# Moving attention steps, weight sums and raw loads by a slot or more, and shifting operand addresses by 32 bytes, in a hand-ordered attention + two-layer MLP kernel

## The chip, the cores and the metric

The kernel runs on one core of a Trainium2 chip. The metric is the device time of one execution in microseconds. The kernel before takes 1599.51 us (median of 3 runs, 1598.06 to 1600.45). Engines are named as in the profile: PE is TensorE, PEld its weight loads, DVE is VectorE, ACT is ScalarE, POOL is GpSimd, SP is SyncE, whose queue here issues most DMAs.

## The reference, cut to what matters

Three stages run one after the other on 4608 rows (8 batches of 576 positions; 8 heads of 64 make 512 columns):

```python
# attention without a score matrix: softmax of q over the head's 64, of k over the 576 positions
q_s = exp(q - max_d q); q_s /= sum_d q_s + 1e-9
k_s = exp(k - max_s k); k_s /= sum_s k_s + 1e-9
x = q_s @ (k_s^T @ v)                      # -> (4608, 512)
# layer 1
h = x @ w_in;  x = (max(h, 0)**2) @ w_out  # 512 -> 2048 -> 512
# layer 2, other weights
h = x @ w_in2; g = where(h > 0, h, exp(min(h, 0)) - 1)
out = g @ w_out2                           # 512 -> 2048 -> 512
```

All of it is float32. The kernel keeps that precision by splitting each operand into a high part (as the matmul rounds it) and the rest: a product is three matmuls, hi x hi, lo x hi and hi x lo.

## The kernel before, in words

The 4608 rows are nine blocks of 512 columns (`TB`). For each block the attention makes x, layer 1 makes h in 16 columns of 128 (`up`, 12 matmuls of 512 each), and then y (`down`). Block 0 runs `up` and `down` by turns and converts the first layer's weights meanwhile. From block 1 on (`PAIRED`), two blocks are a pair: the first block's `up`, the second block's `up`, and then one combined w_out product in 56 units of six matmuls (`u_mm`), a Strassen-like scheme with seven products in place of eight that needs sums and differences of w_out's quarters. Those are made on the chip by `w_join` and `s_first` to `s_lo`, eight groups in the order `FREED`, and stored to DRAM (`w1s`) for `u_load`. The raw weights of layer 2 are loaded in blocks 3 to 8 (`w_load`), put together (`w_scale`, `w_fields`, `w_sign`) and treated in the same way (`w2s`, `w3s`). Layer 2 then runs over five stretches of columns (512, 512, 512, 384, 384): 56 products of six matmuls each in a first phase (`product`, L839: x's halves stream past the weights), and 56 units in a second (`d_mm`, L944: g's halves are the weights and w2 streams).

The order of the work is written out by hand. Every engine does its own instructions strictly in the order in which the program gives them, and waits at the head of its queue. The program's clock is the slot: `(t, "u", j)` is the end of column j of block t, `(0, "c", s)` a half column of block 0, `(t, "s", u)` two units of the combined product. `attention(t)` gives 32 lists of steps, in the order in which they depend on each other; `place_all` spreads these lists over slots, and the loops over `FREED` and over the weights add the sums and the loads by a counter `at` into a list `late` of slots. When a slot comes, its steps are issued on their engines in the order in which they were placed.

What the steps are called: `q_norm` (L367) is the last step on q for one of four row groups; `x_tr` (L380) transposes all four groups of q for one pair of heads, so that it needs the fourth `q_norm`; `x_mm` (L405) multiplies that with `kvs`; `kv_mm` (L288) makes `kvs` for one pair of heads. `xl` and `xh` (L422, L423) are x's two parts for the next block's `up`, `x_split`. `psh` has two PSUM buffers: `up` of column j+2 needs ACT's eviction of column j (L570).

Buffers that the change touches: `st`, four tiles of 2 KB that the sums (`s_hi`, `s_lo`), `y_out` and two `u_load`s share; `raw`, three tiles that raw weights and sums take by turns; `w2`, a ring of nine tiles for layer 2's weights; and the tiles of x's parts (`x2_split`) and g's parts (`d_split`) in layer 2. The last are 64 elements larger than their data, and the data starts at an offset that differs from tile to tile: 32 bytes times the operand's number for x, 0, 64 or 128 bytes for g's high parts, and 32 more for the low ones.

Of the kernel before, what the change touches and what calls it, by code (L numbers as in the profile page):

```python
# [20 lines left out]
def tile_attention_moe_moe2(  # L21
# [171 lines left out]
    def s_hi(w, j, k):  # L193
        hi = pool.tile([P, DM], F32R, tag="st", bufs=4, name=f"sh{w}_{j}_{k}").rearrange("p (i n) -> p i n", n=HW)
        if k == 3:
            nc.scalar.activation(hi[:, 0], s_alone(w, j)[0], AF.Copy)
        else:
            x, d = s_source(w, j, k)
            nc.scalar.activation(hi, x, AF.Copy)
            nc.gpsimd.dma_start(d[:, :, 0, :], f32(hi))  # L200
        parts[w, j, k] = hi

    def s_lo(w, j, k):
# [5 lines left out]
        else:  # L209
            x, d = s_source(w, j, k)  # L210
            lo = pool.tile([P, DM], F32R, tag="st", bufs=4, name=f"sl{w}_{j}_{k}").rearrange("p (i n) -> p i n", n=HW)
# [223 lines left out]
    def attention(t):  # L435
# [6 lines left out]
        for b in new:  # L442
            for p in range(NP):
                for i, f in (
# [3 lines left out]
                    put(i + 4 * p, f, b, p)  # L448
# [7 lines left out]
        turns = ((25, 28), (26, None), (29, 31), (30, None)) if far else ((23, 26), (24, None), (27, 29), (28, None))  # L456
# [128 lines left out]
    def down(layer, t, j):  # L585
# [3 lines left out]
        for c in range(NP):  # L589
# [6 lines left out]
            if last and t < NB - 1:  # L596
                y_out(t, c, pool.tile([P, TB], F32, tag="st", bufs=4, name=f"o{layer}_{t}_{c}"))
# [53 lines left out]
    def u_load(t, u):  # L651
        if u < NU:
            i, j = SEVEN[u // NG][0], u % NG
            tag, bufs = ("at", 2) if u < 2 else ("st", 4) if u < 4 else (("xh", "xl")[u % 2] + str(u % 8 // 2), 1)
# [96 lines left out]
    RING = 9  # L751
# [37 lines left out]
    def shifted(pool, tag, bufs, name, n, o):  # L789

        t = pool.tile([P, 2 * TB + 64], F32R, tag=tag, bufs=bufs, name=name)
        return t[:, o : o + 2 * SIZES[n]].rearrange("p (i n) -> p i n", i=2)
# [3 lines left out]
    def x2_split(n, i):  # L796
        x = xq[n, OPERANDS[i]]
        hi = shifted(early2, f"xh{i}", 1, f"x2h{n}_{i}", n, 8 * i)
        lo = shifted(early2, f"xl{i}", 1, f"x2l{n}_{i}", n, 8 * i)
# [257 lines left out]
    with tc.manual_schedule():  # L1057
# [23 lines left out]
        place_all(x[2:], firsts[PAIRED][:-2])  # L1081
# [19 lines left out]
        late = [(0, "c", s) for s in (NSL - 2, NSL - 1)]  # L1101
        late += sorted(firsts[1] + firsts[1][1::2], key=lambda x: x[2]) + firsts[2][:6]
# [150 lines left out]
```

## Time and profile before

| What | us |
|---|---|
| Median of 3 runs | 1599.51 |
| The profiled execution | 1603.41 |
| Its span, first to last instruction | 1601.5 |
| Around the span (1603.41 - 1601.5) | 1.9 |
| PE busy | 1549.7 (97%) |
| DVE busy | 1227.0 (77%) |
| ACT busy | 1026.0 (64%) |

The profile is of one execution. Busy times of PE overlap (a matmul's recorded time is longer than the distance to the next one's start), so that PE's rate is read from the distance between starts. The stretches of the program, by the starts of their first matmuls: block 0 from 32.7 us, block 1 from 133.9, block 2 from 203.6, the pair's combined product 250.9 to 333.2, blocks 3 and 4 from 333.2, 5 and 6 from 520.2, 7 and 8 from 707.8, the last combined product 805.1 to 882.7, and layer 2 from there to 1597.5, with phases of 77.9 and 80.3 us for 512 columns.

### The profile page before, as it was taken

What the parts mean: (1) busy time and instruction counts of PE and PEld (TensorE: products, weight loads), DVE (VectorE), ACT (ScalarE), POOL (GpSimd) and SP (SyncE); (2) the same over time, 40 slices, a digit from 0 to 9 for tenths busy, and PEclk for the clock granted to TensorE, in tenths of its full rate; (3) what the DMA queues carried; (4) which work ended last, traced back from release to release, by engine and by line L of the source; (5) the groups of instructions that cost most, each with busy time, mean ns of one, the idle gap of its engine ahead of it and who ended that gap; (6) DMA issues with size and microseconds to landing.
All of it is one profiled execution on the core that took longest, in us unless ns stands there. A gap on an engine that the chain in (4) does not pass through costs nothing.

```text
span 1601.5 us, 25635 instructions
## 1 busy us (share of the span) xinstructions
PE 1549.7 (97%) x9046; PEld 1328.0 (83%) x9046; DVE 1227.0 (77%) x1795; ACT 1026.0 (64%) x1648; POOL 107.5 (7%) x214
## 2 busy tenths in 40 slices
PE   5999799999999999999999999999999999999999
PEld 3777587877877777787878889988998899999999
DVE  7986676787878868686488688868876887787786
ACT  7986555567655765666556685478547854875863
POOL 0001220013101230012200000000000000000000
PEclk9999999999999999999999999999999999999999
DMA  9856664856668775656277676777677767888877
GB/s 238 249 173 210 225 233 144 273 191 229 223 183 272 244 248 196 199 198 219 115 253 240 181 241 183 224 204 243 181 224 203 229 183 226 269 273 277 262 238 221
DMA packets 203647, 352.99 MB, mean 220 GB/s; under 512 B 20224, under 2 KB 67328, under 8 KB 203520
## 3 DMA queue, kind: packets, MB, share of 16 engines
q1 hardware_dynamic: 192000, 313.60, 64.3%
q0 software_dynamic: 11520, 37.76, 5.9%
q8 instruction: 73, 1.20, 0.3%
q14 instruction: 54, 0.44, 0.1%
HBM read 288.36 MB, written 62.91 MB: 219 GB/s over the span
## 4 chain that ended last, share of the span: by engine, by line
PE 59%; issue 19%; DVE 11%; ACT 4%; DMA 3%; POOL 2%; SPq 0%; POOLq 0%; DVEq 0%; ACTq 0%
PE p L839 19%; PE y L944 17%; PE p L678 8%; PE ph L562 4%; PE ph L561 4%; PE ph L563 4%; DVE dl L925 2%; DVE t L899 1%; DVE g L903 1%; ACT dh L924 1%; ACT t L890 1%; PE px L405 1%; DVE g L917 1%; PE pt L380 1%; DVE ul L666 1%
## 5 line engine op out<-in xcount | busy, mean ns | idle before, releaser
L944 PE MATMUL y<-w,dh 128*128 128x256 f32 x2016 | 359.4, 281 | 0.0
L839 PE MATMUL p<-x2h,w 128*128 128x512 f32 (+1 forms) x1120 | 325.5, 371 | 0.0
L944 PEld LDWEIGHTS y<-w,dh 128*128 128x128 f32 x2016 | 310.2, 188 | 0.1
L944 PE MATMUL y<-w,dl 128*128 128x256 f32 x1008 | 285.9, 284 | 2.5 <-DVE dl L925 2.2
L678 PE MATMUL p<-uh,w 128*128 128x512 f32 x896 | 282.2, 392 | 0.0
L561 PE MATMUL ph<-xh,wi0h 128*128 128x512 f32 x576 | 232.7, 404 | 4.3 <-ACT B L570 3.6
L839 PEld LDWEIGHTS p<-x2h,w 128*128 128x128 f32 x1120 | 207.3, 188 | 29.5
L562 PE MATMUL ph<-xl,wi0h 128*128 128x512 f32 x576 | 227.4, 395 | 2.0 <-DVE xl L423 1.9
L563 PE MATMUL ph<-xh,wi0l 128*128 128x512 f32 x576 | 227.3, 395 | 1.8 <-DVE wi0l L146 1.8
L839 PE MATMUL p<-x2l,w 128*128 128x512 f32 (+1 forms) x560 | 207.8, 371 | 0.0
L678 PEld LDWEIGHTS p<-uh,w 128*128 128x128 f32 x896 | 168.2, 188 | 36.2 <-issue 1.5
L944 PEld LDWEIGHTS y<-w,dl 128*128 128x128 f32 x1008 | 190.3, 189 | 5.3 <-DVE dl L925 4.8
L665 ACT ACTIVATE uh<-B 128x512 fp32r<-128x512 f32 x192 | 121.0, 632 | 100.9 <-PE p L678 69.8
L924 ACT ACTIVATE dh<-g 128x1024 fp32r<-128x1024 f32 (+1 forms) x120 | 115.7, 973 | 101.5 <-PE y L944 100.5
L678 PE MATMUL p<-ul,w 128*128 128x512 f32 x448 | 176.1, 393 | 2.2 <-DVE ul L666 1.7
L666 DVE TENSOR_TENSOR ul<-B,uh 128x512 fp32r<-128x512 f32 x192 | 130.0, 688 | 52.4 <-ACT uh L665 51.3
L925 DVE TENSOR_TENSOR dl<-g,dh 128x1024 fp32r<-128x1024 f32 (+1 forms) x120 | 133.7, 1115 | 42.3 <-ACT dh L924 41.9
L570 ACT ACTIVATE B<-ph 128x512 f32<-128x512 f32 x128 | 75.9, 593 | 113.9 <-PE ph L563 113.1
L561 PEld LDWEIGHTS ph<-xh,wi0h 128*128 128x128 f32 x576 | 110.8, 192 | 33.9 <-ACT B L570 6.2
L563 PEld LDWEIGHTS ph<-xh,wi0l 128*128 128x128 f32 x576 | 109.5, 190 | 25.9 <-DVE wi0l L146 2.2
L562 PEld LDWEIGHTS ph<-xl,wi0h 128*128 128x128 f32 x576 | 109.9, 191 | 25.4 <-DVE xl L423 3.3
L839 PEld LDWEIGHTS p<-x2l,w 128*128 128x128 f32 x560 | 105.2, 188 | 14.5
(133 smaller groups left out, 2277.2 us busy)
## 6 DMA issues: line engine op xcount, KB each, us to landing
w<-w2s SPq DMA_DIRECT2D x280, 256.0 KB, 3.1
w<-w3s SPq DMA_DIRECT2D x280, 256.0 KB, 3.0
w<-w1s SPq DMA_DIRECT2D x224, 256.0 KB, 3.6
raw_wo<-wo_dram SPq DMA_DIRECT2D x32, 512.0 KB, 4.2
ks<-k_dram SPq DMA_DIRECT2D x32, 320.0 KB, 5.1
vr<-v_dram SPq DMA_DIRECT2D x32, 320.0 KB, 6.1
kt<-kt_dram SPq DMA_DIRECT2D x32, 288.0 KB, 4.4
q<-q_dram SPq DMA_DIRECT2D x36, 256.0 KB, 4.9
```

The source lines that it names most:

```text
L380: nc.tensor.transpose(pt[:, s * P : (s + 1) * P], st["q", t, s][:, 2 * p : 2 * p + 2, :].rearrange("p h d -> p (h d)"), ident,)
L561: nc.tensor.matmul(ph, hi[:, c], xh[p], start=(p == 0), stop=False)
L562: nc.tensor.matmul(ph, hi[:, c], xl[p], start=False, stop=False)
L563: nc.tensor.matmul(ph, lo[:, c], xh[p], start=False, stop=(p == NP - 1))
L570: nc.scalar.activation(g, ph, AF.Relu)
L665: nc.scalar.activation(hi, x, AF.Copy)
L666: nc.vector.tensor_tensor(lo, x, f32(hi), op=ALU.subtract)
L678: nc.tensor.matmul(accs[side, m], w[:, s, m], x, start=(new and (j, s) == (0, 0) and x is hi), stop=(j == NG - 1 and s == 1), skip_group_c ...
L839: nc.tensor.matmul(acc, w[:, s, c], x[:, k], start=(begin and (k, s) == (0, 0) and x is hi), stop=((k, s) == (1, 1)), skip_group_check=not ...
L924: nc.scalar.activation(hi, x, AF.Copy)
L925: nc.vector.tensor_tensor(lo, x, f32(hi), op=ALU.subtract)
L944: nc.tensor.matmul(y2[side, b][:, a * HW : (a + 1) * HW], x[:, u % 2, at], w[:, s], start=(new and (j, s, a) == (0, 0, 0) and x is hi), st ...
```

## The change

It has five parts. (1) Attention for block 1: the last `kv_mm` and the first `x_tr` come a half column later in block 0. Attention for block 2: its last seven lists are no longer spread evenly over block 1, but put on given columns. (2) w_out's sums: one step a slot over block 1 and block 2's first 14 columns, where block 1 had one step in even and two in odd columns and block 2 only six. (3) Layer 2's raw weights: `w_load` a slot later, and no weight steps in the last two columns of blocks 3, 5 and 7; what stood there moves on. (4) `st` has five buffers and the ring `w2` eleven. (5) x's parts in layer 2 have tiles of just their size, which start at multiples of 128 bytes; g's parts all start 32 bytes after a multiple of 64.

```diff
     def s_hi(w, j, k):
-        hi = pool.tile([P, DM], F32R, tag="st", bufs=4, name=f"sh{w}_{j}_{k}").rearrange("p (i n) -> p i n", n=HW)
+        hi = pool.tile([P, DM], F32R, tag="st", bufs=5, name=f"sh{w}_{j}_{k}").rearrange("p (i n) -> p i n", n=HW)
...
-                    put(i + 4 * p, f, b, p)
+                    put(i + 4 * p + (not far and i == 11 and p == NP - 1), f, b, p)
...
-        turns = ((25, 28), (26, None), (29, 31), (30, None)) if far else ((23, 26), (24, None), (27, 29), (28, None))
+        turns = ((25, 28), (26, None), (29, 31), (30, None)) if far else ((24, 26), (24, None), (27, 29), (28, None))
...
-    RING = 9
+    RING = 11
...
-    def shifted(pool, tag, bufs, name, n, o):
-
-        t = pool.tile([P, 2 * TB + 64], F32R, tag=tag, bufs=bufs, name=name)
-        return t[:, o : o + 2 * SIZES[n]].rearrange("p (i n) -> p i n", i=2)
+    def shifted(tag, name, n):
+
+        t = pool2.tile([P, 2 * TB + 16], F32R, tag=tag, bufs=3, name=name)
+        return t[:, 8 : 8 + 2 * SIZES[n]].rearrange("p (i n) -> p i n", i=2)
...
-        hi = shifted(early2, f"xh{i}", 1, f"x2h{n}_{i}", n, 8 * i)
-        lo = shifted(early2, f"xl{i}", 1, f"x2l{n}_{i}", n, 8 * i)
+        hi = early2.tile([P, 2, SIZES[n]], F32R, tag=f"xh{i}", name=f"x2h{n}_{i}")
+        lo = early2.tile([P, 2, SIZES[n]], F32R, tag=f"xl{i}", name=f"x2l{n}_{i}")
...
-        hi = shifted(pool2, "gh", 3, f"dh{n}_{q}", n, 16 * (q % 3))
-        lo = shifted(pool2, "gl", 3, f"dl{n}_{q}", n, 16 * (q % 3) + 8)
+        hi = shifted("gh", f"dh{n}_{q}", n)
+        lo = shifted("gl", f"dl{n}_{q}", n)
...
         place_all(x[:2], [(0, "c", NSL - 2)])
-        place_all(x[2:], firsts[PAIRED][:-2])
+        place_all(x[2:25], firsts[PAIRED][:-5])
+        for s, steps in zip((0, 0, 0, 1, 2, 2, 3), x[25:]):
+            place_all([steps], firsts[PAIRED][NFC - 5 + s :])
...
-        late = [(0, "c", s) for s in (NSL - 2, NSL - 1)]
-        late += sorted(firsts[1] + firsts[1][1::2], key=lambda x: x[2]) + firsts[2][:6]
+        late = [(0, "c", s) for s in (NSL - 2, NSL - 1)] + firsts[1] + firsts[2][:-2]
...
             if t % 2:
-                late += firsts[t]
+                late += firsts[t][:-2]
...
-                    for d, f in ((0, w_load), (3, w_scale), (4, w_fields), (5, w_sign)):
+                    for d, f in ((1, w_load), (3, w_scale), (4, w_fields), (5, w_sign)):
```

Three places where the order of instructions changes. PE, block 0, around column 12 (`pk` is `kv_mm`'s result, `pt` that of `x_tr`, `ph` that of `up`). Before:

```order
L595 MATMUL y_0_3_563<-gh_0_9_1059,wo_9_1082 128x512
L288 MATMUL pk_3_1202<-vr_3_1003,ks_3_1000 64x65 x10
L380 MATMUL pt_0_1225<-ident,q_0_452 128x128
L380 MATMUL pt_0_1225<-ident,q_1_454 128x128
L380 MATMUL pt_0_1225<-ident,q_2_462 128x128
L380 MATMUL pt_0_1225<-ident,q_3_468 128x128
L561 MATMUL ph_0_12_1235<-xh_0_0_384,wi0h_1115 128x512
L562 MATMUL ph_0_12_1235<-xl_0_0_397,wi0h_1115 128x512
```

The same place now, behind the whole of column 12's `up`:

```order
L562 MATMUL ph_0_12_1210<-xl_0_3_423,wi0h_1115 128x512
L563 MATMUL ph_0_12_1210<-xh_0_3_416,wi0l_1116 128x512
L288 MATMUL pk_3_1228<-vr_3_1003,ks_3_1000 64x65 x10
L380 MATMUL pt_0_1252<-ident,q_0_452 128x128
L380 MATMUL pt_0_1252<-ident,q_1_454 128x128
L380 MATMUL pt_0_1252<-ident,q_2_462 128x128
L380 MATMUL pt_0_1252<-ident,q_3_468 128x128
L380 MATMUL pt_1_1259<-ident,q_0_452 128x128
```

The product `pk_3` and the transposes `pt_0` have moved from ahead of column 12's twelve matmuls to behind them, next to `pt_1`.

DVE, block 1, ahead of the fourth `q_norm` (`q_3<-q_3,qz_3`), which the first `x_tr` needs; `mt_wo_j` is `w_join` of row group j of w_out, `sumswo` and `slwo` are the sums and their low parts. Before:

```order
L176 TENSOR_TENSOR sumswo_7_1841<-mt_wo_15_1836,sumswo_7_1841 128x256
L212 TENSOR_TENSOR slwo_7_1_1888<-sumswo_7_1841,shwo_7_1_1885 128x512
L354 TENSOR_REDUCE qz_3_1908<-q_3_1462 128x8
L359 TENSOR_SCALAR qz_3_1908<-qz_3_1908 128x8
L212 TENSOR_TENSOR slwo_7_2_1914<-sumswo_7_1841,shwo_7_2_1911 128x512
L153 TENSOR_TENSOR mt_wo_0_1917<-wo_0_464 128x512
L153 TENSOR_TENSOR mt_wo_8_1919<-wo_8_1008 128x512
L303 TENSOR_SCALAR kz_3_1952<-pk_3_1940 64x1
L304 TENSOR_SCALAR kz_3_1952<-pk_3_1940 64x1
L315 RECIPROCAL kz_3_1952<-kz_3_1952 128x1
L363 RECIPROCAL qz_3_1908<-qz_3_1908 128x8
L367 TENSOR_TENSOR q_3_1462<-q_3_1462,qz_3_1908 128x512
```

The same place now:

```order
L176 TENSOR_TENSOR sumswo_6_1815<-mt_wo_14_1779,sumswo_6_1815 128x256
L212 TENSOR_TENSOR slwo_6_1_1862<-sumswo_6_1815,shwo_6_1_1859 128x512
L354 TENSOR_REDUCE qz_3_1884<-q_3_1462 128x8
L212 TENSOR_TENSOR slwo_6_2_1889<-sumswo_6_1815,shwo_6_2_1886 128x512
L359 TENSOR_SCALAR qz_3_1884<-qz_3_1884 128x8
L303 TENSOR_SCALAR kz_3_1921<-pk_3_1909 64x1
L304 TENSOR_SCALAR kz_3_1921<-pk_3_1909 64x1
L315 RECIPROCAL kz_3_1921<-kz_3_1921 128x1
L363 RECIPROCAL qz_3_1884<-qz_3_1884 128x8
L367 TENSOR_TENSOR q_3_1462<-q_3_1462,qz_3_1884 128x512
L153 TENSOR_TENSOR mt_wo_7_1927<-wo_7_936 128x512
L153 TENSOR_TENSOR mt_wo_15_1929<-wo_15_1406 128x512
```

The sums have reached group 6 here, where they had reached the first step of group 0 (the fifth in the order 4, 5, 6, 7, 0, ...) before: ten DVE instructions fewer stand ahead of that `q_norm` in block 1 (two pairs of L153, four sums, two low parts).

DVE at the start of block 4 (`xl_4_p<-xf_4,xh_4_p` are the low parts that block 4's first `up` needs; `mt_wi_3` and `slwi_2` are steps on layer 2's weights). Before:

```order
L207 TENSOR_TENSOR shwi_2_3_3986<-mt_wi_10_3912,shwi_2_3_3986 128x256
L212 TENSOR_TENSOR slwi_2_1_4011<-sumswi_2_3948,shwi_2_1_4008 128x512
L126 SCALAR_TENSOR_TENSOR mt_wi_3_4014<-raw_wi_3_3882 128x512
L423 TENSOR_TENSOR xl_4_0_4021<-xf_4_0_3909,xh_4_0_4020 128x512
L423 TENSOR_TENSOR xl_4_1_4028<-xf_4_0_3909,xh_4_1_4027 128x512
```

The same place now:

```order
L176 TENSOR_TENSOR sumswi_2_3948<-mt_wi_2_3848,sumswi_2_3948 128x256
L207 TENSOR_TENSOR shwi_2_3_3984<-mt_wi_10_3910,shwi_2_3_3984 128x256
L423 TENSOR_TENSOR xl_4_0_4013<-xf_4_0_3907,xh_4_0_4012 128x512
L423 TENSOR_TENSOR xl_4_1_4020<-xf_4_0_3907,xh_4_1_4019 128x512
L423 TENSOR_TENSOR xl_4_2_4027<-xf_4_2_3980,xh_4_2_4026 128x512
```

The low part `slwi_2_1` and `mt_wi_3` no longer stand between block 3's work and block 4's `xl`; blocks 6 and 8 start in the same way.

## Rows read from the trace of the kernel before

**Rows 1.** The page: busy time of each engine.
```profile
PE 1549.7 (97%) x9046; PEld 1328.0 (83%) x9046; DVE 1227.0 (77%) x1795; ACT 1026.0 (64%) x1648; POOL 107.5 (7%) x214
```

**Rows 2.** Timeline of PE, block 0, column 12: start, duration, instruction, idle time before.
```profile
100.80 0.39 PE L595 MATMUL y<-gh,wo 128*128 128x512 f32 x1
102.43 0.80 PE L288 MATMUL pk<-vr,ks 128*64 128x65 f32 x20 [1.24 <-issue]
105.33 0.48 PE L380 MATMUL pt<-ident,q 128*128 128x128 f32 x1 [1.62 <-DVE q L367]
```

**Rows 3.** Stretches: length, busy time (count) by engine, granted clock, DMA share, GB/s.
```profile
105.40:110.70 5.30, 5.30 (x13) 4.06 (x14) 3.44 (x9) 5.07 (x10) 0.00 (x0) 0.50 0.53 158
181.40:186.30 4.90, 4.90 (x13) 3.88 (x14) 1.35 (x4) 0.60 (x1) 0.00 (x0) 0.51 0.06 23
203.60:250.90 47.30, 47.05 (x258) 37.99 (x257) 35.66 (x73) 26.53 (x52) 7.59 (x20) 1.00 0.51 172
707.80:760.60 52.80, 49.92 (x225) 38.88 (x224) 37.39 (x71) 33.01 (x61) 15.07 (x22) 0.97 0.62 217
882.70:960.50 77.80, 77.80 (x337) 63.12 (x336) 56.77 (x60) 61.23 (x76) 0.00 (x0) 1.00 0.73 217
```

**Rows 4.** Timeline of DVE, block 0: the fourth q_norm.
```profile
104.59 0.68 DVE L367 TENSOR_TENSOR q<-q,qz 128x512 f32<-128x512 f32 x1
```

**Rows 5.** Timeline of PE, block 1: its waits.
```profile
165.54 0.50 PE L561 MATMUL ph<-xh,wi0h 128*128 128x512 f32 x1 [1.58 <-ACT B L570]
169.61 0.80 PE L288 MATMUL pk<-vr,ks 128*64 128x65 f32 x20 [1.04 <-issue]
176.73 0.80 PE L288 MATMUL pk<-vr,ks 128*64 128x65 f32 x20 [0.58 <-issue]
181.37 0.48 PE L380 MATMUL pt<-ident,q 128*128 128x128 f32 x1 [3.37 <-DVE q L367]
191.71 0.66 PE L380 MATMUL pt<-ident,q 128*128 128x128 f32 x4 [0.81 <-ACT xf L416]
196.96 1.09 PE L405 MATMUL px<-qt,kvs 64*64 64x128 f32 x14 [1.04 <-ACT qt L386]
```

**Rows 6.** Groups of DVE by line and form: busy us, mean ns, idle before.
```profile
L153 DVE TENSOR_TENSOR mt_wo<-wo 128x512 f32<-128x512 f32 x16 | 10.3, 682 | 0.0
L166 DVE TENSOR_TENSOR sumswo<-mt_wo,mt_wo 128x256 f32<-128x256 f32 x16 | 6.8, 422 | 0.4
L212 DVE TENSOR_TENSOR slwo<-sumswo,shwo 128x512 fp32r<-128x512 f32 x32 | 21.9, 688 | 30.2 <-ACT shwo L199 24.9 <-DMA w3s<-shwo 3.3 <-DMA w1s<-slwo 1.8
```

**Rows 7.** Timeline of PE, blocks 4, 6, 7 and 8: waits.
```profile
388.97 0.50 PE L562 MATMUL ph<-xl,wi0h 128*128 128x512 f32 x1 [0.84 <-DVE xl L423]
574.62 0.50 PE L561 MATMUL ph<-xh,wi0h 128*128 128x512 f32 x1 [0.56 <-ACT xh L422]
738.65 0.33 PE L380 MATMUL pt<-ident,q 128*128 128x128 f32 x1 [1.92 <-DVE q L367]
761.61 0.50 PE L562 MATMUL ph<-xl,wi0h 128*128 128x512 f32 x1 [0.58 <-DVE xl L423]
```

**Rows 8.** DMA issues by line: count, KB, median us to landing.
```profile
raw_wo<-wo_dram SPq DMA_DIRECT2D x32, 512.0 KB, 4.2
```

**Rows 9.** Timeline of PE, layer 2's first products: low parts of the first two.
```profile
882.91 0.39 PE L839 MATMUL p<-x2l,w 128*128 128x512 f32 x1
883.59 0.39 PE L839 MATMUL p<-x2l,w 128*128 128x512 f32 x1
884.28 0.40 PE L839 MATMUL p<-x2l,w 128*128 128x512 f32 x1
884.98 0.40 PE L839 MATMUL p<-x2l,w 128*128 128x512 f32 x1
```

**Rows 10.** Groups of PE, layer 2's second phase, by form.
```profile
L944 PE MATMUL y<-w,dh 128*128 128x256 f32 x2016 | 359.4, 281 | 0.0
L944 PE MATMUL y<-w,dl 128*128 128x256 f32 x1008 | 285.9, 284 | 2.5 <-DVE dl L925 2.2
```

More of the change, by code (lines that the diff above doesn't have):

```diff
@@ L210, in s_lo @@
             x, d = s_source(w, j, k)
-            lo = pool.tile([P, DM], F32R, tag="st", bufs=4, name=f"sl{w}_{j}_{k}").rearrange("p (i n) -> p i n", n=HW)
+            lo = pool.tile([P, DM], F32R, tag="st", bufs=5, name=f"sl{w}_{j}_{k}").rearrange("p (i n) -> p i n", n=HW)
             nc.vector.tensor_tensor(lo, x, f32(hi), op=ALU.subtract)
@@ L596, in down @@
             if last and t < NB - 1:
-                y_out(t, c, pool.tile([P, TB], F32, tag="st", bufs=4, name=f"o{layer}_{t}_{c}"))
+                y_out(t, c, pool.tile([P, TB], F32, tag="st", bufs=5, name=f"o{layer}_{t}_{c}"))
     def y_out(t, c, o):
@@ L653, in u_load @@
             i, j = SEVEN[u // NG][0], u % NG
-            tag, bufs = ("at", 2) if u < 2 else ("st", 4) if u < 4 else (("xh", "xl")[u % 2] + str(u % 8 // 2), 1)
+            tag, bufs = ("at", 2) if u < 2 else ("st", 5) if u < 4 else (("xh", "xl")[u % 2] + str(u % 8 // 2), 1)
             w = pool.tile([P, 2, 2, P], F32R, tag=tag, bufs=bufs, name=f"w1_{t}_{u}")
```

## The prediction

> **What bounds the kernel now.** I read the page's busy times first: PE is busy 97% of the span, DVE 77% [rows 1]. So a microsecond in which PE stands still, or runs at half its clock, is nearly always a microsecond of the end, and work of DVE or ACT costs only where PE has to wait for it. The timeline of PE was therefore searched for idle times in brackets, and the table of stretches for a granted clock under 1. The reader is to see three kinds of loss. In block 0, PE waits 1.24 us ahead of the last `kv_mm` and 1.62 us for the fourth `q_norm` [rows 2]; then thirteen matmuls take 5.30 us at a granted clock of 0.50 [rows 3], which is the 1.2 GHz level. In block 1 there are six waits, the longest of 3.37 us, again for a `q_norm` [rows 5], and behind it 4.90 us at 0.51 [rows 3]. And the second blocks of pairs start late by 0.84, 0.56 and 0.58 us, for `xl` or `xh` [rows 7]. Layer 2 has no wait of that size: what counts there is the distance from one matmul to the next.
>
> The working is made against the profiled execution: 1603.4 us, span 1601.5 and 1.9 around it. It is 3.9 us above the median of 1599.5; the same difference is then taken from the median.
>
> **Part 1a, block 0.** The two waits are 2.86 us. At full clock three matmuls of 512 columns stand 0.68 us apart (882.91 to 883.59) [rows 9], so twelve need 2.72 us; the slow stretch takes 5.30, a loss of 2.6. After the change column 12's twelve matmuls come first: they would start at 101.03 (0.23 behind the L595 of 100.80), end at 103.76, `kv_mm` takes some 0.73 more, and the fourth transpose is due at about 104.7. The fourth `q_norm` ends at 104.59 + 0.68 = 105.27 [rows 4]. A wait of 0.6 stays. Nothing is added: the transposes are the same ones, and `x_mm` for them keeps its slot. I take 2.86 + 2.6 - 0.6 = **-4.9**; if the clock still falls it is -2.3.
>
> **Parts 1b and 2, block 1.** The six waits are 1.58 + 1.04 + 0.58 + 3.37 + 0.81 + 1.04 = 8.4 us [rows 5], and the slow stretch costs 4.90 - 2.72 = 2.2 [rows 3]; 10.6 in all. The first four waits, 6.6 us, come from DVE being late: its sums stand between attention's steps. Ahead of the fourth `q_norm`, ten instructions go: 4 x 0.68 + 4 x 0.42 + 2 x 0.69 = 5.8 us [rows 6]. So 0.8 of the 6.6 stays. The last two, 0.81 and 1.04, are `x_tr` and `x_mm` treading on each other's two PSUM buffers; with a column of twelve matmuls (2.7 us) between them, ACT's copies fit. The second `x_mm` comes a column later, nearer to block 2's `x_split`: I count 0.5 for that. 10.6 - 0.8 - 0.5 = **-9.3**.
>
> The sums aren't gone: two of the eight groups move into block 2. A group costs DVE 2 x 0.68 + 4 x 0.42 + 2 x 0.69 = 4.4 us, so block 2's DVE goes from 35.66 us to about 44.5 of 47.3 [rows 3], 94%. Not shown before: what such a fill costs there. Bounds: 0 (block 2 today has PE busy 47.05 of 47.30) and 8.8 (block 1's DVE waits with their slow clock, all over again). Nearer is block 2 itself, where every step of attention has columns to spare: **+1**.
>
> **Part 3, raw weights.** Ahead of block 4's `xl`, DVE loses one L212 and one L126, about 1.4 us, more than the waits of 0.84, 0.56 and 0.58 [rows 7]; blocks 6 and 8 are alike: **-2.0**. The steps that left the last two columns stand elsewhere, and every later one shifts. Block 7's wait of 1.92 us on a `q_norm` [rows 7] and the clock of 0.97 over 52.8 us there (1.6 us) [rows 3] may go or be copied into block 5. Bounds -7 and +5; with the fifth `st` buffer, which takes away DVE's 3.3 and 1.8 us behind DMAs [rows 6], I take **-2**. A raw load now has two slots, 5.4 us, to land, and a median of 4.2 us [rows 8]: that cover is 1.2 us thick. It was issued into a queue that stood still until DVE freed the buffer, so that it will hardly land later: 0. SP's order behind it (k, v and w1 loads) only gets freer.
>
> **Part 4.** A ring of nine covers nine products of 1.39 us already: 0. The two extra loads stand at the end of a stretch in which PE is full.
>
> **Part 5a, x's parts.** The first product's operand starts at a multiple of 128 bytes, the second's 96 bytes after one: their low parts' triples take 0.68 and 0.70 us [rows 9]. The whole phase runs at 77.8 / 336 = 231.5 ns a matmul [rows 3], the aligned product at 227. If all 1008 matmuls of 512 columns came down to 227, it would be -4.6; if the first product is quick for another reason, 0. No row shows a gain at 384 columns. Midway: **-2.3**. On the Trainium skill, SBUF — State Buffer, "Operand start alignment", an operand need only start at a multiple of its element size, and the same page gives cachelines of 16 bytes, in which 32 is as good a start as 0; by that this term is 0 and the sum 17.2. The pair 0.68 and 0.70 speaks against it, thinly.
>
> **Part 5b, g's parts.** All of them will start 32 bytes off, as only the low parts do now. Matmuls with a low part show 284 ns, with a high one 281 [rows 10]. If 3 ns is the price of an offset, 2016 x 3 = +6 us; if it is the price of going from one offset to the other, 1008 x 3 = -3. Recorded durations are not distances, and both kinds of term are gone if the difference is only in the record: **0**.
>
> **Sum.** -4.9 - 9.3 + 1 - 2.0 - 2 - 2.3 = -19.5: 1583.9 for an execution like the profiled one, **1580.0** for the median.
>
> **Rivals.**
> 1. The clock falls at other waits. For it: a wait of 1.92 us in block 7 is enough company for a fall, and small waits will stay. Against: both long slow stretches come straight behind the longest waits. It gives back 2.6 + 2.2: 1584.8. On the Trainium skill, TensorE: Matmul & The Clock Gate, Part 1, the unit that watches PE runs freely, so that equal work can meet it differently from run to run; no run here shows that yet.
> 2. Block 2 becomes what block 1 was: DVE at 94% of it, PE waiting for `kv_mm` and `x_tr` in its columns 6 to 13. For it: the same steps, the same engine. Against: its attention steps are spread thinner and it has no `down`. It puts back 8.8 in place of 1: 1587.8.
> 3. g's parts at 32 bytes cost their 6 us: 1586.0. For it: 284 against 281; against: it is 1% of a modelled duration.
> 4. Slower: the raw loads. There are 32 in blocks 3 to 8. If each lands after its `w_scale` is due, ACT stands at the head of its queue with the evictions of `ph` behind it, and PE has two buffers. Above 0.61 us of PE a load (19.5 / 32) the gain is gone; at 1 us it is 1580 + 32 = 1612. Against: 5.4 us for 4.2, and ACT is busy 64% [rows 1].
> 5. That the change doesn't do what it says would be an address that is not moved: then part 5 is 0, inside the forecast's range.
>
> **How the numbers follow.** The forecast gets 0.55, with a range of its own of 1574 to 1586; rival 1 0.18, rival 2 0.15, rival 3 0.07, rival 4 0.05. All but the last are well over 0.2% (3.2 us, about what a measurement of this kernel can tell from no change) faster; two together, or rival 2 doubled, could reach 1596.3, for which 0.03 is set aside out of rivals 2 and 3. So faster 0.92, within 0.2% 0.03, slower 0.05. The range of 1571 to 1592 takes in rivals 1 to 3; its lower end has part 3 at -7 and x's parts at -4.6 with a little over (-26.8, 1572.7).
>
> **What would show it.** Right: no bracket of a `q_norm` over 1 us on PE in blocks 0 and 1; granted clock 1.0 from about 100 to 200 us; block 2 starting some 14 us earlier; `xl` and `xh` not named at the starts of blocks 4, 6 and 8; layer 2's first phases of 512 columns at about 77.1 us, the second ones still 80.3. Wrong: brackets of 1 us and more in block 2's columns 6 to 13, or a DMA of raw weights named ahead of L120 on ACT and PE waiting behind; a second phase of 81 us or more; or a clock under 1 at a new place.

## The result: 1585.47 us, 0.9915 of the time before

The changed kernel takes 1585.47 us (median of 4 runs, 1582.64 to 1589.17) against 1599.45 us for the kernel before: a ratio of 0.9915, 95% interval 0.9891 to 0.9938. The forecast was 1580.0, with a range of 1571 to 1592. The profiled execution took 1583.97 us with a span of 1582.0, and the sum made for the profiled execution was 1583.9. That agreement is chance: one term was wrong by 8.7 us and others made up for it. Lengths by the starts of the first matmuls, each profile against its own start:

| Stretch | before | after | difference | the prediction's term |
|---|---|---|---|---|
| block 0 | 101.18 | 104.99 | +3.8 | -4.9 (1a) |
| block 1 | 69.65 | 59.11 | -10.5 | -9.3 (1b and 2) |
| block 2 | 47.29 | 46.72 | -0.6 | +1 |
| combined product behind it | 82.37 | 82.33 | 0 | 0 |
| blocks 3 to 8 with their products | 549.46 | 542.79 | -6.7 | -4.0 (3) |
| layer 2, five first phases | 350.93 | 345.02 | -5.9 | -2.3 (5a) |
| layer 2, five second phases | 363.89 | 364.18 | +0.3 | 0 (5b) |

Each length is that of one execution. Experiments that keep the old code in a stretch show how far such a length moves: block 0 takes 99.9 to 102.6 us in eight executions, block 1 68.5 to 69.7 in four, blocks 3 to 8 with their products 546.4 to 549.5 in five.

### The profile page after: what moved, and what is told of

It reads as the page before. It is cut to its first block, busy times and chain, and to the rows that moved or that the text cites. A ratio compares the mean times of both kernels' runs of the same rounds, so it can differ in the third digit from the quotient of the medians.

```text
span 1582.0 us, 25637 instructions
## 1 busy us (share of the span) xinstructions
PE 1539.0 (97%) x9046; PEld 1324.4 (84%) x9046; DVE 1224.6 (77%) x1795; ACT 1025.9 (65%) x1648; POOL 107.4 (7%) x214
## 4 chain that ended last, share of the span: by engine, by line
PE 76%; DVE 12%; ACT 5%; DMA 2%; issue 2%; SPq 0%; DVEq 0%; ACTq 0%
PE p L839 20%; PE y L944 18%; PE p L678 16%; PE ph L561 6%; PE ph L563 6%; PE ph L562 6%; DVE dl L925 2%; DVE ul L666 1%; DMA raw_wi<-wi_dram 1%; PE px L405 1%; DMA raw_wo<-wo_dram 1%; PE pt L380 1%; ACT dh L924 1%; PE pk L288 1%; DVE g L903 1%
## 5 line engine op out<-in xcount | busy, mean ns | idle before, releaser
L839 PE MATMUL p<-x2h,w 128*128 128x512 f32 (+1 forms) x1120 | 321.5, 367 | 0.0
L665 ACT ACTIVATE uh<-B 128x512 fp32r<-128x512 f32 x192 | 120.8, 632 | 99.9 <-PE p L678 71.3
L570 ACT ACTIVATE B<-ph 128x512 f32<-128x512 f32 x128 | 76.0, 595 | 110.8 <-PE ph L563 109.0
```

Source lines behind the costliest of these rows:

```text
L570: nc.scalar.activation(g, ph, AF.Relu)
L839: nc.tensor.matmul(acc, w[:, s, c], x[:, k], start=(begin and (k, s) == (0, 0) and x is hi), stop=((k, s) == (1, 1)), skip_group_check=not ...
```

## The profile after

The page of the kernel after gives PE 10.7 us less of busy time, at the same share of a shorter span, as in [rows 1]:

```profile
PE 1539.0 (97%) x9046; PEld 1324.4 (84%) x9046; DVE 1224.6 (77%) x1795; ACT 1025.9 (65%) x1648; POOL 107.4 (7%) x214
```

The stretches of the kernel after, from the same view as [rows 3] (start and end, length, busy time and count of each engine, granted clock, DMA share, GB/s): the slow part of block 0, block 1, block 2, blocks 3 to 8 with their combined products, block 5 alone, and one phase of each kind of layer 2.

```profile
110.40:117.20 6.80, 4.88 (x14) 4.01 (x15) 4.62 (x8) 5.71 (x11) 0.00 (x0) 0.52 0.47 154
137.81:196.92 59.11, 57.68 (x350) 45.47 (x348) 37.01 (x86) 37.09 (x72) 12.40 (x24) 1.00 0.64 225
196.92:243.64 46.72, 46.72 (x257) 38.05 (x256) 40.88 (x86) 27.89 (x55) 12.34 (x26) 1.00 0.66 228
325.98:868.77 542.79, 533.98 (x2721) 426.12 (x2719) 418.18 (x722) 333.85 (x610) 80.89 (x140) 1.00 0.67 221
511.28:566.48 55.20, 52.33 (x324) 41.03 (x323) 41.48 (x88) 38.62 (x77) 15.08 (x25) 1.00 0.72 238
868.77:944.94 76.17, 76.17 (x338) 63.09 (x336) 56.32 (x60) 61.24 (x76) 0.00 (x0) 1.00 0.75 221
944.94:1025.41 80.47, 80.01 (x673) 79.68 (x672) 68.38 (x64) 42.63 (x45) 0.00 (x0) 1.00 0.72 202
```

Of the three slow parts of [rows 3] one is left, and it stands later in block 0. Blocks 1 and 2 are at full clock, block 2 with PE busy from end to end and DVE at 40.88 of 46.72. The first phase of layer 2 is 1.7 us shorter, the second one has not moved. Block 1 keeps one wait, not for a `q_norm` but for ACT's L311, which reads `kv_mm`'s result (`pk`) out of PSUM:

```profile
182.11 0.66 PE L380 MATMUL pt<-ident,q 128*128 128x128 f32 x4 [1.43 <-ACT kvs L311]
```

The timeline of PE in block 0 of the kernel after (start, duration, instruction, idle time before and its releaser) shows the new loss at the place of [rows 2]:

```profile
104.36 0.80 PE L288 MATMUL pk<-vr,ks 128*64 128x65 f32 x20
105.09 0.66 PE L380 MATMUL pt<-ident,q 128*128 128x128 f32 x4
112.32 1.11 PE L380 MATMUL pt<-ident,q 128*128 128x128 f32 x4 [6.58 <-ACT kvs L311]
113.66 0.63 PE L594 MATMUL y<-gl,wo 128*128 128x512 f32 x1
117.50 0.40 PE L594 MATMUL y<-gl,wo 128*128 128x512 f32 x1
```

The waits of 1.24 and 1.62 us are gone, as forecast. But the next transposes, `pt_1`, wait 6.58 us for ACT's L311: attention has two PSUM buffers, `pt_0` is in one, and the other still holds `pk_3` until L311 has read it out. From there nine matmuls take 3.84 us (113.66 to 117.50) at half clock. The timeline of ACT says why L311 is late:

```profile
105.11 0.69 ACT L120 ACTIVATE raw_wi<-raw_wi 128x512 f32<-128x512 f32 x1 [1.01 <-DMA raw_wi<-wi_dram]
109.07 0.57 ACT L570 ACTIVATE g<-ph 128x512 f32<-128x512 f32 x1
110.50 0.68 ACT L120 ACTIVATE raw_wi<-raw_wi 128x512 f32<-128x512 f32 x1 [0.19 <-DMA raw_wi<-wi_dram]
111.62 0.65 ACT L311 ACTIVATE kvs<-pk,kz 64x64 f32<-64x64 f32 x2
120.92 0.60 ACT L570 ACTIVATE g<-ph 128x512 f32<-128x512 f32 x1 [4.65 <-PE ph L563]
```

ACT runs some 5 to 6 us behind PE here, with hardly a gap: column 12's matmuls end at 104.4 and its L570 starts at 109.07, `pk_3` ends at 105.2 and L311 starts at 111.62. L311 moved a slot with `kv_mm`, and so stands behind the next column's L570, L572, L120 and L121; in the kernel before it came at 109.48, now at 111.62. The last row is the other half of the circle: as PE stood, ACT then waits 4.65 us for PE.

In block 5 a wait of 0.71 us in the kernel before, for DVE, grows to 2.36, for ACT. PE before; then ACT and PE of the kernel after:

```profile
549.64 0.80 PE L288 MATMUL pk<-vr,ks 128*64 128x65 f32 x20 [0.71 <-DVE slwi L212]
```

```profile
539.26 0.67 ACT L120 ACTIVATE raw_wi<-raw_wi 128x512 f32<-128x512 f32 x1 [2.18 <-DMA raw_wi<-wi_dram]
541.50 0.83 ACT L279 ACTIVATE ks<-ks 128x512 f32<-128x512 f32 x2
```

```profile
542.23 0.80 PE L288 MATMUL pk<-vr,ks 128*64 128x65 f32 x20 [2.36 <-ACT ks L279]
```

A raw load lands 2.2 us after ACT has come to it, `k_exp` (L279) stands behind it, and PE waits 2.36 us for that. Over blocks 3 to 8 ACT waits 9.5 us for raw loads in five places; the trace before has no such wait of ACT there. In blocks 3 and 7 PE waits up to 0.96 us for an eviction (L570) that stands behind such a load. The `xl` and `xh` of [rows 7] no longer hold up the starts of blocks 4, 6 and 8.

## Experiment 1: block 0's steps back where they were

```diff
-                    put(i + 4 * p + (not far and i == 11 and p == NP - 1), f, b, p)
+                    put(i + 4 * p, f, b, p)
...
-        turns = (...) if far else ((24, 26), (24, None), (27, 29), (28, None))
+        turns = (...) if far else ((23, 26), (24, None), (27, 29), (28, None))
```

> The changed kernel with block 0's attention steps put back where the kernel before has them (part 1a undone, all else kept). Theory: in the changed kernel three users of the two PSUM buffers of attention (pk_3, pt_0, pt_1) stand in a row on PE, and the third waits 6.58 us for ACT's L311, with 6.8 us at half clock behind it; with the steps apart again block 0 comes back from 105.0 to about 101.2 us, with the old waits of 1.24 and 1.62 us, and the kernel gets 3.8 us faster than the changed one: 1581.7. Rival: the 6.58 us come from raw weights that land late (ACT's L120 waits 1.0 us for a DMA in both kernels); then the wait stays somewhere in block 0, its length stays near 105, and the time near 1585.5.

Measured: 1581.79 us, a ratio of 0.9890 to the kernel before (0.9877 to 0.9904), 3.7 us under the changed kernel. Block 0 takes 100.40 us. The theory holds: part 1a costs 3.7 us where it was to bring 4.9. The intervals of this ratio and of the changed kernel's overlap a little, but the stretch does not leave it to them: in eight executions with the old order block 0 takes 99.9 to 102.6, with the changed one 105.0.

## Experiments 2 and 3: how far apart the users of the two buffers must stand

Second transpose a half column later:

```diff
-        ... ((24, 26), (24, None), (27, 29), (28, None))
+        ... ((24, 26), (25, None), (27, 29), (28, None))
```

> The changed kernel with the second x_tr of block 0 a half column later (slot 25 in place of 24), so that a down of twelve matmuls, 2.7 us, stands between pt_0 and pt_1. Theory (pt_1 waits for its PSUM bank until ACT's L311 has read pk_3 out at about 112.3): the wait of 6.58 shrinks by 2.7 to 3.9 us, and some or all of the 6.8 us at half clock (3.2 us lost) stay or go with it: block 0 between 99.0 and 102.3, the time 1579.5 to 1582.8. Rival: what is late is ACT itself, waiting for raw weights; then PE loses the same time at a later place of block 0, its length stays at 104 to 105, and the time at 1585.

Measured: 1584.38 us (0.9904, 0.9888 to 0.9921), block 0 102.36. PE's wait in the timeline:

```profile
113.67 1.11 PE L380 MATMUL pt<-ident,q 128*128 128x128 f32 x4 [4.33 <-ACT kvs L311]
```

The wait shrinks by 2.25 of the 2.7 us and names the same releaser, and block 0 gives back 2.6; the half clock behind it stays. The mechanism is right, but the median fell by 1.1 us only, nearer to the rival's time. In the profiled execution the rest of block 0's gain is lost at places that this edit does not touch: the first matmul starts 1.3 us later than in the changed kernel's, and the last combined product takes 78.85 us for 77.57.

With `kv_mm` back in slot 23 as well:

```diff
-                    put(i + 4 * p + (not far and i == 11 and p == NP - 1), f, b, p)
+                    put(i + 4 * p, f, b, p)
```

> The changed kernel with kv_mm back in slot 23 (as before), the first x_tr in slot 24 (as changed) and the second in slot 25: one user of attention's two PSUM buffers in each slot. Theory: pk_3 waits 1.24 us as in the kernel before, L311 comes at about 109.5 as there, pt_0 has no wait, pt_1 waits about 1.1 us, and the clock stays up: block 0 at 97 to 99 us, the time 1577.5 to 1580. Rival: the clock falls at the short waits all the same, 2 to 3 us are lost again, and the time is that of block 0 as before, 1581.8.

Measured: 1582.56 us (0.9892, 0.9877 to 0.9907), block 0 103.14. The timeline of PE and the stretch from 110 to 120 us:

```profile
102.38 0.80 PE L288 MATMUL pk<-vr,ks 128*64 128x65 f32 x20 [1.20 <-issue]
110.66 0.65 PE L380 MATMUL pt<-ident,q 128*128 128x128 f32 x4 [1.30 <-ACT kvs L311]
116.70 1.80 PE L405 MATMUL px<-qt,kvs 64*64 64x64 f32 x14 [2.31 <-ACT qt L386]
```

```profile
110.00:120.00 10.00, 7.04 (x36) 4.38 (x37) 7.18 (x11) 9.90 (x20) 0.00 (x0) 0.85 0.45 157
```

The first two waits are as forecast; the third is new, and behind it the clock falls (0.85 over these 10 us), where the theory had it stay up. So the forecast of 1577.5 to 1580 missed, and the rival's time, 1581.8, is the nearer one. In this execution the clock also falls in block 5 (56.41 us, against 54.62 in experiment 2). ACT is busy 9.90 of 10 us: in these columns it is the engine that is late, and the order on PE only chooses at which instruction PE meets that.

## Experiment 4: x's parts aligned, alone

The kernel before with this, nothing else:

```diff
-        hi = shifted(early2, f"xh{i}", 1, f"x2h{n}_{i}", n, 8 * i)
+        hi = early2.tile([P, 2, SIZES[n]], F32R, tag=f"xh{i}", name=f"x2h{n}_{i}")
...
```

> The kernel before with x's parts in layer 2 alone aligned (part 5a). Theory: every matmul of a first phase of 512 columns, not only those of the first product, stands closer to the next; phases of 512 go from 77.9 to 76.2 us and those of 384 from 58.6 to 58.2, in all -5.9 us: 1593.6. Rival (the prediction): half of the matmuls gain, -2.3 us: 1597.2. Rival: the first phases of the changed kernel are quicker for the deeper ring of w2 tiles; then nothing changes here: 1599.5.

Measured: 1594.44 us (0.9968, 0.9956 to 0.9980), -4.8 by the medians; the first phase of layer 2:

```profile
880.84:957.00 76.16, 76.16 (x337) 63.08 (x336) 56.24 (x60) 61.23 (x76) 0.00 (x0) 1.00 0.73 221
```

76.16 as in the changed kernel; the ring of eleven has no part in it. All five first phases together are 5.9 us shorter, and both the phases and the median (interval -7.0 to -3.2) rule out -2.3.

## Experiment 5: one common start for all of x's parts

```diff
-        hi = shifted(early2, f"xh{i}", 1, f"x2h{n}_{i}", n, 8 * i)
-        lo = shifted(early2, f"xl{i}", 1, f"x2l{n}_{i}", n, 8 * i)
+        hi = shifted(early2, f"xh{i}", 1, f"x2h{n}_{i}", n, (8, 16, 4, 8, 16)[n])
+        lo = shifted(early2, f"xl{i}", 1, f"x2l{n}_{i}", n, (8, 16, 4, 8, 16)[n])
```

> The kernel before with one common offset for all of x's parts in layer 2, another in each stretch of columns: 32, 64, 16, 32 and 64 bytes behind a multiple of 128. A stretch of 512 columns takes 76.2 us where all start at a multiple of 128 bytes, 77.9 where the starts differ. Theory 1: the start itself counts: 32 and 16 bytes cost as much as they do in the kernel before (233 ns a matmul, 78.3 us the stretch), 64 bytes some 229 ns, 76.9 us. Theory 2: only the step from one start to another counts: all three stretches take 76.2 us, and those of 384 columns 58.2.

The five first phases of this kernel (one run, 1598.1 us), in the view of stretches:

```profile
877.45:955.86 78.41, 78.41 (x338) 62.97 (x337) 56.88 (x60) 61.24 (x76) 0.00 (x0) 1.00 0.73 215
1036.27:1113.18 76.91, 76.91 (x338) 63.10 (x337) 56.17 (x59) 61.23 (x76) 0.00 (x0) 1.00 0.76 226
1193.68:1271.51 77.83, 77.83 (x338) 63.18 (x337) 56.42 (x59) 61.22 (x76) 0.00 (x0) 1.00 0.74 217
1351.95:1411.31 59.36, 59.36 (x338) 59.36 (x337) 43.66 (x59) 48.25 (x76) 0.00 (x0) 1.00 0.88 283
1472.65:1530.89 58.24, 58.24 (x338) 58.24 (x337) 43.57 (x59) 48.24 (x76) 0.00 (x0) 1.00 0.84 265
```

Theory 1 holds to 0.1 us in the first two, 78.41 for 32 bytes and 76.91 for 64; 16 bytes cost less than it had (77.83 for 78.3). Divided by 336 matmuls that is 233.4, 228.9 and 231.6 ns, against 226.7 aligned. At 384 columns 32 bytes cost 59.36 and 64 bytes nothing (58.24, as aligned). So theory 2 is out: with one common start there is no step from one start to another, and the start costs time all the same.

That the step adds nothing, and that every multiple of 128 bytes is free, is not shown. In the first phases of the kernel before, by the starts of each operand's matmuls (means of the three phases of 512 columns), the operand that starts 128 bytes into its tile takes 231.5 ns a matmul where the one at 0 takes 228.2, and the one at 192 takes 232.4 where the one at 64 takes 229.2. At 384 columns the operand at 32 bytes takes 174.0 there and 176.7 here. Where the tiles themselves start in memory is in no trace.

## Experiments 6 and 7: block 1's part alone, and the sums alone

The kernel before with the sums one step a slot and the last seven lists of attention on given columns; then with the sums alone (the first hunk):

```diff
-        late += sorted(firsts[1] + firsts[1][1::2], key=lambda x: x[2]) + firsts[2][:6]
+        late = [(0, "c", s) for s in (NSL - 2, NSL - 1)] + firsts[1] + firsts[2][:-2]
...
-        place_all(x[2:], firsts[PAIRED][:-2])
+        place_all(x[2:25], firsts[PAIRED][:-5])
+        for s, steps in zip((0, 0, 0, 1, 2, 2, 3), x[25:]):
+            place_all([steps], firsts[PAIRED][NFC - 5 + s :])
```

> The kernel before with w_out's sums put one step a slot over blocks 1 and 2, and the last seven lists of block 2's attention put on given columns of block 1 (parts 1b and 2), and nothing else. Theory: block 1 goes from 69.7 to about 59.1 us and block 2 stays at 47, in all -11.1: 1588.4. Rival (the prediction's working): -9.3 and block 2 +1, 1591.2. Rival: part of the gain needs block 0's change or the fifth st buffer; then block 1 stays above 62 us and the time above 1591.

Measured: 1593.04 us (0.9961, 0.9948 to 0.9973). The two blocks, and PE in the product behind them:

```profile
134.81:193.92 59.11, 57.68 (x350) 45.46 (x349) 37.11 (x86) 37.22 (x72) 12.40 (x24) 1.00 0.64 225
193.92:240.64 46.72, 46.72 (x257) 38.03 (x256) 40.88 (x86) 27.90 (x55) 12.35 (x26) 1.00 0.65 219
```

```profile
246.28 0.47 PE L678 MATMUL p<-uh,w 128*128 128x512 f32 x1 [1.40 <-DMA w<-w1s]
```

Blocks 1 and 2 come out exactly as in the changed kernel, so they need nothing of its other parts. The median falls by 6.2 only. One microsecond goes again at once: the sums now end later, and with four `st` buffers the product waits for its weights (83.38 us in place of 82.3). In the changed kernel, with five buffers, this wait is not there, so part 4, which I had put at 0, is probably worth that 1 us beside part 2; no run has the five buffers with this part alone. The rest of the difference between -11.1 and -6.2 I cannot place: the profiled execution of the kernel before has 52.85 us for block 7 where the four others with the same code there have 49.6 to 51.0, and the first matmul stands at 32.1 to 34.3 us from one execution to another, so that a difference of two profiles says less than that of a stretch.

> The kernel before with only w_out's sums spread one step a slot over blocks 1 and 2 (part 1's second half of block 2's attention stays as it was). Theory (the prediction's split): four of block 1's six waits go with the sums, 5.8 us and the slow clock behind them; the two for x_tr and x_mm, 0.81 and 1.04 us, stay: block 1 at 61 us in place of 59.1. Rival: the sums' waits stay in part, since the fourth q_norm still stands where it stood; block 1 at 63 us or more.

Measured in one run: 1592.3 us, block 1 60.91. The waits of PE that are left in block 1:

```profile
173.63 0.33 PE L380 MATMUL pt<-ident,q 128*128 128x128 f32 x1 [0.97 <-DVE q L367]
181.78 0.66 PE L380 MATMUL pt<-ident,q 128*128 128x128 f32 x4 [0.81 <-ACT xf L416]
187.04 1.09 PE L405 MATMUL px<-qt,kvs 64*64 64x128 f32 x14 [1.04 <-ACT qt L386]
```

This is the prediction's working, wait by wait: of the `q_norm` wait 0.97 stays (I had 0.8), and 0.81 and 1.04 are the last two of [rows 5] unchanged.

## Experiment 8: the raw weights' part alone

The kernel before with `w_load` a slot later, the last two columns of blocks 3, 5 and 7 free, and five `st` buffers.

```diff
-                late += firsts[t]
+                late += firsts[t][:-2]
...
-                    for d, f in ((0, w_load), (3, w_scale), (4, w_fields), (5, w_sign)):
+                    for d, f in ((1, w_load), (3, w_scale), (4, w_fields), (5, w_sign)):
```

> The kernel before with the raw weights' loads a slot later, no weight steps in the last two columns of blocks 3, 5 and 7, and five st buffers (part 3 and half of part 4), and nothing else. Theory: blocks 4, 6, 7 and 8 get 1.2, 3.4, 2.6 and 0.9 us shorter, block 5 0.8 and the combined product behind block 6 1.1 us longer, in all some -6.6 us: 1592.9; the 3.4 us of half clock in block 7 are gone. Rival (the prediction): -4: 1595.5. Rival: the clock's fall in block 7 comes and goes from run to run and isn't the edit's; then block 7 keeps it here, and the gain is about 4 us or less.

Measured: 1596.71 us (0.9981, 0.9972 to 0.9990), -2.6. Blocks 3 to 8 with their products, and PE in block 5:

```profile
333.96:876.54 542.58, 534.32 (x2721) 425.98 (x2720) 418.05 (x722) 333.62 (x610) 80.91 (x140) 1.00 0.66 220
```

```profile
549.87 0.80 PE L288 MATMUL pk<-vr,ks 128*64 128x65 f32 x20 [1.99 <-ACT ks L279]
```

The same stretch takes 546.4 to 549.5 in the five executions with the code of the kernel before there (the profile before and experiments 4 to 7), and 542.6 to 544.8 in the six with this part's code (the changed kernel, experiments 1 to 3, 8 and 10): 4.4 between the middles, 1.6 to 6.9 between the ends. The theory's -6.6 missed. It had counted 2.6 us for block 7, whose slow clock was chance, as the second rival said: of the five executions only the profile before has it. The wait for `ks` in block 5 comes with this part.

By the medians the three parts alone bring 4.8, 6.2 and 2.6 us, together 13.6; the kernel of experiment 1, which has them all without part 1a, is 17.5 us faster than the kernel before. One of the 3.9 us between may be the wait for weights in experiment 6; the others are not placed.

## Experiments 9 to 11: the raw loads back at their old slot

Experiment 1's kernel with one number undone:

```diff
-                    for d, f in ((1, w_load), (3, w_scale), (4, w_fields), (5, w_sign)):
+                    for d, f in ((0, w_load), (3, w_scale), (4, w_fields), (5, w_sign)):
```

> The changed kernel with block 0's attention as before (so to be held against the 1581.8 us of that) and with the raw loads back at their old slot; the two free columns at the end of blocks 3, 5 and 7 and the five st buffers stay. In the changed kernel ACT waits 2.18 us in block 5 for a raw load (L120), k_exp (L279) stands behind it, and PE waits 2.36 us there for kv_mm; with a fall of the clock behind that wait in some executions block 5 takes 54.6 to 57.1 us, against 54.4 before. Theory: with the load a slot earlier ACT's wait goes, block 5 is back at 54.4, blocks 4, 6 and 8 keep their gains, which come from the free columns: 1579 to 1581. Rival (the prediction's reason for the later load): issued early, the load stands in SP's queue until its buffer comes free, holds up the loads behind it, and blocks 4, 6 and 8 go back part of the way: 1583 or more.

Measured: 1575.20 us (0.9845, 0.9830 to 0.9860), the fastest of all and clear of the changed kernel's interval. That is also some 4 us under the theory's 1579 to 1581, which counted block 5 alone. Stretches of it (100 to 120 us, block 5, blocks 3 to 8 with their products), then ACT and PE in block 5:

```profile
100.00:120.00 20.00, 15.48 (x98) 11.36 (x98) 15.90 (x29) 18.49 (x36) 0.00 (x0) 1.00 0.49 156
507.37:560.66 53.29, 52.07 (x325) 41.09 (x323) 41.28 (x88) 38.88 (x77) 15.08 (x25) 1.00 0.63 222
321.86:862.14 540.28, 533.41 (x2721) 426.22 (x2719) 417.88 (x722) 334.11 (x610) 80.87 (x140) 1.00 0.66 222
```

```profile
533.08 0.67 ACT L120 ACTIVATE raw_wi<-raw_wi 128x512 f32<-128x512 f32 x1
535.64 0.83 ACT L279 ACTIVATE ks<-ks 128x512 f32<-128x512 f32 x2
```

```profile
536.37 0.34 PE L288 MATMUL pk<-vr,ks 128*64 128x65 f32 x4 [1.05 <-ACT ks L279]
```

ACT has no wait for a raw load left in blocks 3 to 8. Block 5 takes 53.29 us; experiment 1 had 57.07, the changed kernel 55.20. Blocks 4 and 8 keep 46.75 and 43.55 us: their gain came from the free columns, and the rival's return of SP's hold-up does not show. Block 7 takes 48.20 in place of 50.15; block 6 alone is longer, 48.37 for 47.18, which experiments 11 and 12, also with early loads, do not repeat (47.2). Blocks 3 to 8 with their products take 539.0 to 540.3 in these three executions, under all six with the later loads.

Two attempts at block 0 stand beside it. In the first, experiment 3's order has its four copies of `pt` on DVE; in the second, that and the early loads:

```diff
-        nc.scalar.activation(qt, pt, AF.Copy)
+        if t == 1:
+            nc.vector.tensor_copy(qt, pt)
+        else:
+            nc.scalar.activation(qt, pt, AF.Copy)
```

> One user of attention's PSUM buffers in each slot (kv_mm in slot 23, x_tr in 24 and 25; 1582.6 us), and the four copies of x_tr's results (L386) that block 0 makes for block 1 on DVE in place of ACT. Theory: between 100 and 120 us ACT is the engine that is late in block 0 (9.9 of 10 us busy from 110 to 120); relieved of 0.6 us a copy, and with DVE free some 2.8 of 10 us there, x_mm's wait of 2.31 us goes and the clock stays up: block 0 shorter by 2.3 to 4 us, the time 1578.5 to 1580.3. Rival: DVE's own queue waits for ACT (gh, 1.6 and 2.1 us at a time), the copies come no earlier, and the time stays at 1582.6.

Measured: 1582.44 us (0.9885, 0.9868 to 0.9901), no gain over experiment 3; the wait has only changed its name:

```profile
117.84 1.09 PE L408 MATMUL px<-qt,kvs 64*64 64x64 f32 x14 [2.46 <-DVE qt L387]
```

> Both edits at once: one user of attention's PSUM buffers in each slot of block 0 with its four copies on DVE, and the raw loads back at their old slot. Theory: the two gains add up, 2.3 to 4 us in block 0 and 0.8 to 2.7 in block 5: 1576 to 1579.5. Rival: block 0's loss only moves to the start of block 1, or the early loads cost what they cost in the kernel before: 1581 or more.

Measured: 1579.07 us (0.9867, 0.9852 to 0.9882). Against the kernel without the early loads, on the same chip, that is -3.4: the later loads cost 3.4 us here, and 6.6 by experiments 1 and 9, which ran on two chips. The time lies in the theory's range by luck: its gain in block 0 did not come (102.65 us, as without the early loads), and the loads' gain was larger than forecast.

## Experiment 12: the last pair of heads a slot earlier

Experiment 9's kernel with one line changed:

```diff
-                    put(i + 4 * p, f, b, p)
+                    put(i + 4 * p - (not far and p == NP - 1), f, b, p)
```

> The version with block 0 as before and the raw loads at their old slot (1575.2 us), with the steps on k for the last pair of heads all one slot earlier in block 0. Theory: pk_3's wait of 1.22 us goes, the fourth q_norm still ends where DVE brings it, and L311 comes a slot earlier in ACT's queue, so that the second x_tr's wait of 1.61 us for it shrinks or goes: 1573.6 to 1575. Rival: ACT is busy 18.5 of 20 us from 100 to 120, what is given first there makes the next thing late, and the time stays at 1575.2.

Measured: 1576.85 us (0.9855, 0.9839 to 0.9872), not faster. PE's wait for `pk_3` is longer, not gone:

```profile
101.75 1.35 PE L288 MATMUL pk<-vr,ks 128*64 128x65 f32 x20 [2.25 <-issue]
```

ACT's `k_exp` came 1.3 us earlier (101.03 for 102.31) and L311 2.2 us (107.83 for 110.01), so that the second `x_tr` no longer waits for it, as the theory said. But PE came to `kv_mm` earlier still, the clock falls there (from 101.5 us), and block 0 takes 101.40 us for 100.34: the rival holds.

## Why the prediction was right in the sum and wrong in a step

**Part 1a is the step that failed.** "Nothing is added" looked at the instructions and not at the buffers: `pk_3`, `pt_0` and `pt_1` use two PSUM buffers in turn, and with all three in one slot the third waits for the first one's eviction. I went by ACT's share of the whole span (64% [rows 1]), although [rows 3] has it at 5.07 of 5.30 us in just these columns; from 100 to 120 us it is busy 92% (18.49 of 20.00, experiment 9), so an eviction moved by a slot comes later. Instead of -4.9 the term is +3.8.

**The term's 2.6 us for the clock were not there to be had either.** In experiment 9 PE has the same two waits as in [rows 2] and the clock stays at 1.00; what comes then is this, from its timeline:

```profile
103.02 0.80 PE L288 MATMUL pk<-vr,ks 128*64 128x65 f32 x20 [1.22 <-issue]
105.98 0.33 PE L380 MATMUL pt<-ident,q 128*128 128x128 f32 x1 [1.69 <-DVE q L367]
110.70 0.66 PE L380 MATMUL pt<-ident,q 128*128 128x128 f32 x4 [1.61 <-ACT kvs L311]
```

PE at full speed arrives early and waits 1.61 us for L311. Block 0 takes 100.34 us, against 101.18 with the slow stretch: half the clock mostly filled that wait. The eight executions with the old order bear it out. In three of them the clock stays up in block 0 (experiments 4, 6 and 9), and in these three alone PE waits for L311, 1.51 to 1.63 us; block 0 takes 100.3 to 100.5 us there, and 99.9 to 102.6 in the five whose clock falls, 0.5 us more on the average.

**Parts 1b and 2** were right in mechanism and to about a microsecond in size (-9.4 to -10.5 for -9.3, by which execution of the old block 1 is taken). What is left in block 1 is not what I had left there, 0.8 for a `q_norm` and 0.5 for block 2's `x_split`, but 1.43 us for L311: the buffers of block 0's miss once more. Block 2 has no price (46.72 us, 87% DVE, no wait), so rival 2 is out; my +1 was pulled up by the upper end of its bounds.

**Part 3** came out at about -4.4 for -4.0, but as a sum of two terms of which I had put one at 0. The free columns, with the fifth `st` buffer, bring some 8 us (539.0 to 540.3 in experiments 9, 11 and 12 against 546.4 to 549.5), and the later loads take 3.4 to 6.6 back by the medians, 3.7 between the middles of this stretch: "it will hardly land later" compared a median of 4.2 us [rows 8] with two slots, and a median says nothing of the few loads that stand behind others. That is rival 4, at a tenth to a fifth of its 32 us and in five loads rather than 32. What I feared would be "copied into block 5", block 7's wait for a `q_norm`, did not come; block 5's wait is another, for `k_exp` behind a raw load. The 1.6 us for block 7's clock were a matter of that one execution. And the largest piece, 3.3 us of block 6 (50.58 to 47.23), I had not priced. Most of it is a wait of `kv_mm` in the kernel before that [rows 7] leaves out; ACT came to `k_exp` late there, behind a weight step (L199) that waits 3.61 us for DVE. In the kernel after it is 0.38 us:

```profile
606.92 0.80 PE L288 MATMUL pk<-vr,ks 128*64 128x65 f32 x20 [2.02 <-issue]
```

**Part 5a** was mis-sized: -5.9 for -2.3, since I took the middle between "all" and "none" at 512 columns and nothing at 384; the gain is 5.1 us at 512 columns, over my "all" of 4.6, and 0.8 at 384. On the Trainium skill, SBUF — State Buffer, "Operand start alignment" gives an operand any start at a multiple of its element size, which is about what is legal and not about time. From the cachelines of 16 bytes on the same page of the Trainium skill the prediction had worked out that 32 bytes is as good a start as 0; the 78.41 and 76.17 us measured here do not agree with that, and the measurement decides.

**Part 5b** was right: second phases of 80.4 to 80.6 us with either starts, so 281 and 284 ns [rows 10] were no price. g's parts are the weights there, and their start costs nothing that can be seen.

**Rival 1**, the clock falling elsewhere, is half true: it falls once more, in block 0, behind a wait of 6.58 us that I had not foreseen.

**Of the signs** named ahead, block 2 starts 6.7 us earlier and not some 14 (196.92 for 203.57), and the clock is not at 1.0 from 100 us on. Two signs of being wrong came: a clock under 1 at a new place, and a raw load named ahead of L120 with PE waiting behind. They belong to parts 1a and 3.

## What to carry to other kernels

Before moving a step past a slot, follow its result to the instruction that frees its buffer, and ask how busy that engine is in just those columns, not over the span. A stretch at half clock, or a wait, may only fill a wait that stands behind it: look at what the next engine would make of the time before counting it as a gain. And start the streaming operand of a matmul at the beginning of its tile (226.7 ns a matmul at 512 columns); 64 bytes into it cost 2.2 ns here, 32 bytes 6.7, and 128 bytes alone were not tried. The weights' start is free here.

## What the runs showed of the hardware

- Streaming fp32r operands of 512 columns that all start 64, 16 or 32 bytes into their tiles (experiment 5) cost 2.2, 4.9 and 6.7 ns a matmul over the 226.7 of operands that fill their tiles; at 384 columns 0 at 64 bytes and 3.3 ns (59.36 for 58.24 over 336) at 32. With mixed starts the kernel before shows other figures, told under experiment 5.
- The clock does not fall behind equal waits equally. In block 5 it stays at 1.00 behind 2.36 us (changed kernel) and falls behind 2.58 (experiment 1). Behind 1.99 us for the same `kv_mm` it falls in experiment 3 and not in experiment 8. Block 5 and the fall in it, first in experiment 1, then the wait and the fall in experiment 3:

```profile
507.92:564.99 57.07, 53.98 (x325) 42.16 (x323) 41.54 (x88) 38.67 (x77) 15.08 (x25) 0.97 0.68 231
536.00:550.00 14.00, 11.42 (x64) 9.04 (x63) 8.81 (x21) 10.38 (x21) 3.47 (x5) 0.88 0.56 198
```

```profile
539.41 0.80 PE L288 MATMUL pk<-vr,ks 128*64 128x65 f32 x20 [1.99 <-ACT ks L279]
539.40:545.50 6.10, 6.09 (x39) 5.01 (x40) 3.90 (x12) 4.21 (x9) 2.89 (x4) 0.72 0.62 228
```

  In block 0 it falls to 0.50 behind waits of 1.24 and 1.62 us [rows 2, 3], and not at all behind 1.22 and 1.69 (experiment 9); of the eight executions with these two waits it falls in five. The Trainium skill, TensorE: Matmul & The Clock Gate, Part 1, has the unit that watches PE run freely, so that the same work can meet it differently; these rows agree with that, where the trace of before alone could not show it.
